# Products with v of two jobs in one group, queries turned by 24 rows, one PSUM bank for transposes

## The chip, the cores and the metric

The kernel runs on one core of one Trainium2 chip. The metric is the device time of one execution in microseconds, as the median of several runs. All times inside an execution come from one profiled execution, counted from the start of its span.

## The reference

Windowed attention with a few global keys feeds a gated feed-forward network. B = 4, H = 8 heads of D = 64, S = 768, d_model 512, d_ff 1024, all float32.

```python
rel = pos[:, None] - pos[None, :]
keep = (pos[None, :] < n_global) | ((rel >= 0) & (rel < n_local))   # 8 and 96
scores = q @ k.T / sqrt(D) - slopes[h] * dist                       # masked where not keep
x = softmax(scores) @ v                                             # heads side by side: 768 x 512
h = relu(x @ w_in)
conv = sum(conv_w[i] * shift(h, i) for i in range(3))               # along the sequence
out = (h * sigmoid(conv)) @ w_out
```

## The kernel before

A **job** is one batch, one half of the sequence (u = 0 or 1, 384 queries) and one pair of heads: 32 jobs. A job has three **steps** of 128 queries, 96 in all; the two heads of the pair are j = 0 and 1. Four jobs make the input x of one **unit** of the feed-forward network (FFN), so there are 8 units.

A step sees at most 232 keys: 96 before its 128 queries, its own 128, and 8 global ones. They stand in a first chunk of 128 (96 + 24 own + 8 global) and a second chunk of 104, the step's own keys 24 to 127. Queries 0 to 23 of a step see no key of the second chunk. The first step of a batch has 128 keys and no second chunk.

The way of one step, with its lines:

- L585 and L586 (L583 for the first nine jobs): scores into a PSUM bank, tile `s`, on TensorE.
- L594: bias, mask and maximum on VectorE, with a table `tab` made at the start from `rel`, the distances.
- L607: exponentials on ScalarE into `pbuf`, one of four buffers (`NPB`). L617 and L621: sum and reciprocal. L630 or L627: normalisation on VectorE, GpSimd or ScalarE.
- L639 and L640, `transposes`: second chunk and first chunk of each head are turned on TensorE into a PSUM bank `t`. There are two such banks, `tbank`, taken in turn. The weights are 104 or 128 columns of `pbuf`, and an identity of 128 columns is what moves. The second chunk is turned first and with all 128 queries, 24 more than it needs; the first chunk then overwrites those 24 columns.
- L646, `evict`: ScalarE copies the bank to one of four tiles `pt` (`NPT`) in SBUF.

After the three steps of a job, `values` (L656) multiplies with v into the one PSUM bank `pv`: for each step and chunk the two heads' weights are 64 columns wide and lie side by side; as fp32 each product is two instructions, 24 in a job and 20 in a job whose first step has one chunk. `high_x` (L666, ScalarE) and `low_x` (L671, VectorE) split the result into two fp32r parts, `xh` and `xl`, with six buffers each.

The FFN of a unit is `mm1` (L684, tile `h`, 3 matmuls of 384 columns for each of 8 x 4 blocks, which read the x of the unit's four jobs as k = 0 to 3), ReLU (L692), a three-tap convolution (L715 or L713, then L717 twice on VectorE), a gate (L725, L732, L749), a split (L756, L767) and `mm2` (L777, tile `o`, 3 matmuls of 512 columns for each of 8 blocks of a tile of rows). The last tile of rows is L805. The FFN's matmuls have a fixed order among themselves: the first layer of a unit (for its first two blocks all k in turn), then the second layer of the unit before.

The order in which each engine works is not written by hand. `fast_path` lists every operation with its engine, cost, buffers, predecessors and due time, and `Plan` places them one after another, by due time among those that are ready. `rooms` says how many buffers of a kind there are. In the first 40 us warm-up matmuls (L363) fill TensorE's gaps; by then the FFN's weights are decoded and split (L516 to L532). v (two buffers), q and k are loaded through SP's queue.

Of the kernel before, what the change touches and what calls it, by code (L numbers as in the profile page):

```python
# [23 lines left out]
P = 128  # L24
# [12 lines left out]

HF, NG = NF // 2, 4
NU, SPU = 2 * B, NPAIR * NB
NPB, NPT, NMM = 4, 4, 6  # L40
OFF = (1, 4)
NATIVE = 9
HK = 1024
# [33 lines left out]
class Plan:  # L77
# [53 lines left out]
    def arrange(self, free, taken):  # L131
# [31 lines left out]
                return min(max(0.0, port["DVE"] - t) * x, c[0] * x / (1 - x))  # L163
            return 0.0

        def room(b):

            t, n = b[0], self.rooms[b[0]]
            if queue[t][0] != b and t not in self.loose:
                return None  # L170
            ln = line.setdefault(t, [])
            if len(ln) < n:
                return 0.0
            old, at = ln[len(ln) - n]
            if old is None:
                return at
            return None if users[old] else gone[old]

        while cand:
            best = None  # L180
            heads = {}
            for k in cand:
                o = ops[k]
                at, ok = 0.0, True
                for b in o.alloc:
                    r = room(b)
                    if r is None:
                        ok = False
                        break
                    at = max(at, r)  # L190
                if not ok:
                    continue
                for a in o.after:
                    at = max(at, end[a])
                for e, c in o.eng.items():
                    t = max(free[e], at + WAKE[e])
                    if k[0] in LOADS:
                        t = max(t, landed[-LANES])
                    if e == "DVE" and last_max and k[0] == "max":
                        t = max(t, free[e] + 130)  # L200
                    late = at + WAKE[e] + (MARGIN[e] if free[e] > EASY else 0)
                    heads.setdefault(e, []).append((max(t, late), o.due, k, c, t))
            if not heads:
                raise RuntimeError(sorted(map(str, cand))[:40])
            pick = None
            for e, hs in heads.items():
                t0 = min(h[0] for h in hs)
                _, due, k, c, t = min((h for h in hs if h[0] <= t0 + SLACK[e]), key=lambda h: (h[1], h[0]))
                if len(ops[k].eng) > 1:
                    mine = t + c[0] + beside(e, c, t) + (c[2] if len(c) > 2 else 0)  # L210
                    others = [
                        h[4] + h[3][0] + beside(x, h[3], h[4]) + (h[3][2] if len(h[3]) > 2 else 0)
                        for x, g in heads.items() if x != e for h in g if h[2] == k
                    ]
                    if others and min(others) < mine:
                        hs = [h for h in hs if h[2] != k]
                        if not hs:
                            continue
                        t0 = min(h[0] for h in hs)
                        _, due, k, c, t = min((h for h in hs if h[0] <= t0 + SLACK[e]), key=lambda h: (h[1], h[0]))  # L220
                if pick is None or t < pick[0]:
                    pick = (t, e, k, c)
            t, e, k, c = pick
            o = ops[k]
            del cand[k]
            if k[0] in LOADS:
                free[e] = t + ISSUE
                wire = max(t + ISSUE + SETUP, wire) + c[0]
                end[k] = wire + RESULT["SP"]
                landed.append(end[k])  # L230
            else:
                cost = c[0] + beside(e, c, t)
                free[e] = t + cost
                end[k] = t + cost + (150 if k[0] == "max" else RESULT[e])
                if e == "POOL" and c[1]:
                    port[e], pool_op = t + cost, k
                if e == "DVE" and c[1] > 1:
                    port["slow"] = BESIDE[k[0]]
                    if port["POOL"] > t:
                        x = port["slow"]  # L240
                        more = min(cost * x, (port["POOL"] - t) * x / (1 - x))
                        port["POOL"] += more
                        free["POOL"] = max(free["POOL"], port["POOL"])
                        end[pool_op] += more
                    port[e] = t + cost
            if e == "DVE":
                last_max = k[0] == "max"
            done.append((t, o, e))
            for b in o.alloc:
                queue[b[0]].remove(b)  # L250
                line.setdefault(b[0], []).append((b, 0.0))
            for b in {*o.alloc, *o.use}:
                users[b] -= 1
                gone[b] = max(gone[b], end[k])
            for x in outs[k]:
                left[x] -= 1
                if not left[x]:
                    cand[x] = None
# [17 lines left out]
def fast_path(tc, io):  # L276
# [13 lines left out]
    px = pool("px", 6)  # L290
    pg = pool("pg", 4)
    ps_s = pool("ps_s", 2, space=PSUM)
    ps_t = pool("ps_t", 2, space=PSUM)
    ps_v = pool("ps_v", 1, space=PSUM)
    ps_m = pool("ps_m", 3, space=PSUM)
    p2 = pool("p2", 2)

# [22 lines left out]
    def load_q(m, j):  # L320
        b, u, hp = jobs[m]
        if m < NATIVE:
            r = slice(D * j, D * j + D)
            E = nc.sync if m + j else nc.scalar
            E.dma_start(raw[m, "q"][r, j * TB : j * TB + TB], io["qt"][b, hp, r, u * TB : u * TB + TB])
        else:
            t = raw[m, "q"] = p1.tile([P, 2 * TB], F32, tag="rq", name=f"rq{m}")
            nc.sync.dma_start(t, io["qk%d" % u][b, hp][:, : 2 * TB])
# [33 lines left out]
        for _ in range(n):  # L362
            T.matmul(wp[0][:, TB : TB + P], wz, wz, start=len(wp) > 1, stop=len(wp) > 1, skip_group_check=len(wp) == 1)  # L363

    tbank = [ps_t.tile([P, 2 * WIN], F32, tag="t", name=f"t{x}") for x in range(2)]
    for t in tbank:
        for c in range(0, 2 * WIN, P):
            w = min(P, 2 * WIN - c)
# [12 lines left out]
    for c0, n, base in pieces:  # L381
        if base is None:
            G.iota(reli[:, c0 : c0 + n], pattern=[[0, n]], base=-1, channel_multiplier=0)
        else:
            G.iota(reli[:, c0 : c0 + n], pattern=[[-1, n]], base=base, channel_multiplier=1)
    keyi = p2.tile([P, NGLOB], I32, tag="pt", name="keyi", bufs=NPT)
    G.iota(keyi, pattern=[[1, NGLOB]], base=0, channel_multiplier=0)
    ident = const.tile([P, P], F32, name="ident")
    V.tensor_copy(rel, reli)
    keyf = p1.tile([P, NGLOB], F32, tag="ob", name="keyf")  # L390
    V.tensor_copy(keyf, keyi)

# [67 lines left out]

    zero_q(0)
    make_identity(nc, ident)
    zero_q(1)

    cw = const.tile([P, 3 * NF], F32, name="cw")
# [166 lines left out]
    def transposes(s, j):  # L632
        n = form(s)[3]
        pb = pbuf[s % NPB]
        if j == 0:
            st_pt[s] = tbank[s % 2]
        pt, c = st_pt[s], j * WIN
        if n > P:
            T.transpose(pt[:NLATE, c + NLATE : c + WIN], pb[:, c + P : c + WIN], ident)  # L639
        T.transpose(pt[:, c : c + P], pb[:, c : c + P], ident)  # L640

    def evict(s):
        sb = p2.tile([P, 2, WIN], F32, tag="pt", name=f"pt{s}", bufs=NPT)
# [5 lines left out]
    def values(m):  # L649
        pv[m] = ps_v.tile([P, TB], F32, tag="v", name=f"pv{m}")  # L650
        for i in (NB - 1, *range(NB - 1)):
            whole = form(NB * m + i)[2]
            sb = st_pt.pop(NB * m + i)
            for c, n, q in ((0, P, 0),) if whole else ((0, P, 0), (1, NLATE, NEAR)):
                for j in range(2):
# [5 lines left out]
                        stop=c == 1 or whole,  # L661
                    )

    def high_x(m):
        xh = px.tile([P, TB], F32R, tag="xh", name=f"xh{m}")
        A.activation(xh, pv[m], AF.Copy)  # L666
        xt[m] = [xh, None]

    def low_x(m):
        xl = px.tile([P, TB], F32R, tag="xl", name=f"xl{m}")  # L670
        V.tensor_tensor(xl, pv[m], xt[m][0].bitcast(F32), ALU.subtract)  # L671
        xt[m][1] = xl

# [190 lines left out]
    def table_on(h, r, eng="DVE"):  # L864
        table(h, r, V if eng == "DVE" else G)

    plan = Plan(dict(s=2, t=2, v=1, m=3, xh=6, xl=6, gh=4, gl=4, rk=1, rq=1, kk=2, ql=2, qh=2,
                     vv=2, pt=NPT, pb=NPB, mm=6, c=1, ob=1), ("ob",))
    add = plan.add
    NRM_POOL, NRM_ACT, TAP_ACT = 300.0, 200.0, 0.0  # L870
# [11 lines left out]
    def due_of(s):  # L882
# [2 lines left out]
            return 8000 + i * PACE0  # L885
        return max(8000 + s * PACE0, starts[n - 1] + (i + 1) / SPU * spans[n - 1] - LEAD)

    for m in range(len(jobs)):
        native, w = m < NATIVE, NKC[jobs[m][1]]
        D0 = due_of(NB * m)  # L890
# [21 lines left out]
        for i in range(NB):  # L912
# [20 lines left out]
                add(("t", s, j), ("PE", (108 if first else 196, 0)), (transposes, s, j), [("nrm", s, j)],  # L933
                    (("t", s),) if j == 0 else (), (("t", s), ("pb", s)), d + 1500 + j, [("t", s, 0)] if j else [])
            add(("ev", s), act(256 if first else 2 * WIN), (evict, s), [("t", s, 0), ("t", s, 1)], (("pt", s),), (("t", s),), d + 2200)
        add(("pv", m), ("PE", (1570 if jobs[m][1] else 1390, 0)), (values, m), [("ev", NB * m + i) for i in range(NB)] + [("ldv", m)],
            (("v", m),), (("vv", m), *(("pt", NB * m + i) for i in range(NB))), d + 3000)
        ss = [("pv", m)]
        add(("xh", m), act(TB), (high_x, m), ss, (("xh", m),), (("v", m),), d + 3500)
        add(("xl", m), ("DVE", (TB * 1.042 + 68, 0)), (low_x, m), [("xh", m)], (("xl", m),), (("xh", m), ("v", m)), d + 3900)  # L940

# [249 lines left out]
def host(q, k, v, n_global, n_local, moe_w_in, moe_conv_w, moe_w_out):  # L1191
    arrays = {}
    qt = q.transpose(0, 1, 3, 2).reshape(B, NPAIR, 2, D, S).transpose(0, 1, 3, 2, 4)
    kt = k.transpose(0, 1, 3, 2).reshape(B, NPAIR, 2, D, S).transpose(0, 1, 3, 2, 4)
    for u in range(2):
        qu = qt[..., u * TB : (u + 1) * TB].reshape(B, NPAIR, D, 2 * TB)
        ku = kt[..., key_columns(u)].reshape(B, NPAIR, D, 2 * NKC[u])
# [12 lines left out]
    vv = vn[:, :, idx]  # L1210
    vv = vv.reshape(B, NPAIR, 2, NB, 2, P, P).transpose(0, 2, 1, 5, 3, 4, 6)
    arrays["vv"] = vv.reshape(B, 2, NPAIR, P, NB * 2 * P)
    arrays["qt"] = q.transpose(0, 1, 3, 2).reshape(B, NPAIR, P, S)
    arrays["kt"] = k.transpose(0, 1, 3, 2).reshape(B, NPAIR, P, S)
    arrays["vn"] = vn
# [25 lines left out]
```

## Time and profile before

| | before |
|---|---|
| median of 3 runs | 429.93 us (429.76 to 430.14) |
| profiled execution | 429.85 us, span 428.1 us |
| TensorE busy | 420.0 us, 98% |
| TensorE weight loads | 375.1 us, 88% |
| VectorE busy | 361.3 us, 84% |
| ScalarE busy | 311.5 us, 73% |
| GpSimd busy | 116.7 us, 27% |
| mean granted TensorE clock | 0.999 |
| chain that ended last | TensorE 57%, VectorE 33% |

Matmuls are pipelined: a row's duration holds the latency, and neighbouring rows overlap. What a matmul costs the engine is the distance from its start to the next start, the pitch. The last 55 us of the span (from 373) are the FFN of the last unit alone.

### The profile page before, as it was taken

The page shows a single profiled execution, that of the slowest core. Times are in us where ns is not written, and L with a number is a line of the kernel's source. Part 1 is how long each engine was busy: PE and PEld are TensorE (multiplying, and loading weights), DVE is VectorE, ACT ScalarE, POOL GpSimd, SP SyncE. Part 2 cuts the span into 40 slices and gives each one's busy share as a digit, 9 for nine tenths or more (in the row PEclk, how much of TensorE's full clock was granted, in tenths as well). Part 3 has the DMA queues.
Part 4 walks back from the last instruction along what each step waited for, and adds up shares of the span by engine and source line. Part 5 has one row for each costly group of instructions (what it writes and reads, how often), then busy time and mean ns, then how long its engine had stood idle before and what let it go on. Part 6 is the DMA issues. An engine that isn't in the chain of part 4 may idle for free.

```text
span 428.1 us, 8754 instructions
## 1 busy us (share of the span) xinstructions
PE 420.0 (98%) x2996; PEld 375.1 (88%) x2996; DVE 361.3 (84%) x1030; ACT 311.5 (73%) x829; POOL 116.7 (27%) x176
## 2 busy tenths in 40 slices
PE   8999999999999999999999999999999999999996
PEld 7999999898899778998799988899789988898885
DVE  7799999999899998889998997789999986568700
ACT  3789998989897885588878856589877886355511
POOL 6554444533213311223321421123203310001000
PEclk9999999999999999999999999999999999999999
DMA  7998544425403344434334323434444123576111
GB/s 254 301 339 281 174 141 154 143 85 160 143 31 123 112 147 113 139 97 148 96 117 123 86 90 105 156 114 124 122 160 129 57 70 116 198 266 224 51 49 54
DMA packets 22513, 59.85 MB, mean 140 GB/s; under 512 B 2880, under 2 KB 5440, under 8 KB 22464
## 3 DMA queue, kind: packets, MB, share of 16 engines
q1 hardware_dynamic: 21952, 58.89, 43.6%
q8 instruction: 24, 0.39, 0.4%
q10 hardware_dynamic: 512, 0.36, 0.3%
q14 instruction: 25, 0.20, 0.1%
HBM read 52.95 MB, written 6.29 MB: 138 GB/s over the span
## 4 chain that ended last, share of the span: by engine, by line
PE 57%; DVE 33%; issue 4%; ACT 4%; DMA 1%; POOL 0%; ACTq 0%; POOLq 0%
PE o L777 21%; PE h L684 17%; DVE c L717 8%; DVE s L594 6%; PE pv L656 5%; DVE kk L341 3%; DVE pbuf L630 3%; DVE c L749 3%; PE t L640 3%; PE s L583 2%; PE t L639 2%; DVE ql L349 2%; DVE gl L767 2%; PE s L586 2%; PE s L585 2%
## 5 line engine op out<-in xcount | busy, mean ns | idle before, releaser
L607 ACT ACTIVATE pbuf<-s,mm 128x232 f32<-128x232 f32 (+1 forms) x192 | 82.7, 437 | 33.3 <-DVE mm L594 32.8
L684 PE MATMUL h<-xh,wih 128*128 128x384 f32 x256 | 93.5, 365 | 0.0
L717 DVE SCALAR_TENSOR_TENSOR c<-hbuf,cw,c 128x382 f32<-128x382 f32 (+1 forms) x128 | 84.1, 673 | 3.4 <-POOL c L715 2.6
L684 PE MATMUL h<-xh,wil 128*128 128x384 f32 x256 | 86.5, 338 | 0.0
L684 PE MATMUL h<-xl,wih 128*128 128x384 f32 x256 | 86.5, 338 | 0.0
L594 DVE CUSTOM_DVE_ANT_0 s<-s,tab 128x232 f32<-128x232 f32 (+1 forms) x192 | 73.2, 381 | 10.6 <-PE s L586 7.1
L777 PE MATMUL o<-woh,gh 128*128 128x512 f32 x184 | 76.5, 416 | 0.0
L777 PE MATMUL o<-woh,gl 128*128 128x512 f32 x184 | 72.9, 396 | 0.0
L777 PE MATMUL o<-wol,gh 128*128 128x512 f32 x184 | 72.8, 396 | 0.0
L646 ACT ACTIVATE pt<-t 128x464 f32<-128x464 f32 (+1 forms) x96 | 50.8, 531 | 12.6 <-PE t L640 12.2
L715 POOL TENSOR_SCALAR c<-hbuf,cw 128x382 f32<-128x382 f32 (+1 forms) x33 | 24.9, 758 | 104.9 <-ACT hbuf L692 89.7
L684 PEld LDWEIGHTS h<-xh,wih 128*128 128x128 f32 x256 | 48.3, 189 | 1.4
L684 PEld LDWEIGHTS h<-xl,wih 128*128 128x128 f32 x256 | 48.4, 189 | 0.2
L684 PEld LDWEIGHTS h<-xh,wil 128*128 128x128 f32 x256 | 48.1, 188 | 0.0
L640 PE MATMUL t<-ident,pbuf 128*128 128x128 f32 x192 | 47.0, 275 | 0.1
L337 POOL CAST kk<-rk 128x1008 fp32r<-128x1008 f32 (+1 forms) x23 | 25.6, 1113 | 77.6 <-PE s L586 45.8
L656 PEld LDWEIGHTS pv<-pt,v 128*64 128x64 f32 (+1 forms) x704 | 36.1, 136 | 8.1 <-issue 4.0
L639 PE MATMUL t<-ident,pbuf 128*104 128x128 f32 x160 | 40.5, 278 | 2.4 <-DVE pbuf L630 2.1
L656 PE MATMUL pv<-pt,v 128*64 128x128 f32 (+1 forms) x704 | 42.5, 267 | 0.0
L777 PEld LDWEIGHTS o<-woh,gl 128*128 128x128 f32 x184 | 34.6, 188 | 8.2
L630 DVE TENSOR_SCALAR pbuf<-pbuf,mm 128x232 f32<-128x232 f32 (+1 forms) x109 | 40.4, 395 | 1.0
L777 PEld LDWEIGHTS o<-woh,gh 128*128 128x128 f32 x184 | 34.8, 189 | 6.0
(105 smaller groups left out, 843.0 us busy)
## 6 DMA issues: line engine op xcount, KB each, us to landing
v<-in_vv SPq DMA_DIRECT2D x32, 384.0 KB, 3.2
rq<-in_qk SPq DMA_DIRECT2D x23, 384.0 KB, 3.6
check<-in_w SPq DMA_DIRECT2D x16, 512.0 KB, 4.2
wr<-in_w SPq DMA_DIRECT2D x16, 511.6 KB, 5.8
rk<-in_qk SPq DMA_DIRECT2D x12, 504.0 KB, 3.5
out<-ob SPq DMA_DIRECT2D x23, 256.0 KB, 2.1
rk<-in_qk SPq DMA_DIRECT2D x11, 400.0 KB, 3.1
rq<-in_qt SPq DMA_DIRECT2D x17, 96.0 KB, 5.0
```

Source lines behind the costliest of these rows:

```text
L337: G.tensor_copy(kk, raw[m, "k"])
L594: V.tensor_tensor_reduce(out=o, in0=o, in1=tab[:, h, WIN:] if first else tab[:, h, 0:WIN], scale=-0.125, scalar=3.0e38, op0=ALU.add, op1=A ...
L607: last_exp[s] = A.activation(weights_of(s, j), st_s[s][:, j, :n], AF.Exp, bias=mm[:, j : j + 1], scale=-1.0, accum_out=mm[:, 2 + 2 * j : 3 ...
L630: X.tensor_scalar(x, x, y, 1.0, ALU.mult, ALU.mult)
L639: T.transpose(pt[:NLATE, c + NLATE : c + WIN], pb[:, c + P : c + WIN], ident)
L640: T.transpose(pt[:, c : c + P], pb[:, c : c + P], ident)
L646: A.activation(sb[:, :, :n], pt[:, :, :n], AF.Copy)
L656: T.matmul(pv[m][64 * j : 64 * j + 64, i * P + q : (i + 1) * P], vt[m][:n, i, c, 64 * j : 64 * j + 64], sb[:n, j, c * P : c * P + P - q], ...
L684: T.matmul(ps[:, :TB], w_[:, k, f * P : (f + 1) * P], x_, start=part == 0 and k == 0, stop=part == 2 and k == NK - 1,)
L715: G.tensor_scalar(c, h, x, 1.0, ALU.mult, ALU.mult)
L717: V.scalar_tensor_tensor(c, h, x, c, ALU.mult, ALU.add)
L777: T.matmul(ps, g_[:, f], w_[:, f], start=f == 0 and part == 0, stop=f == NF - 1 and part == 2,)
```

## The change

Queries of each step are turned by 24 rows: the host orders them 24 to 127, 0 to 23. The queries that see the second chunk then stand in rows 0 to 103, so its transposes take 104 rows and move an identity of 104 columns. The first chunk is turned with an identity that is turned too, which puts the queries back in order. The distances of the mask follow: `wrap` takes 128 from the rows from 104 on.

From job 8 on, the products with v of jobs 8 and 9, 10 and 11, and so on are one operation of the plan, which waits for the evictions of both jobs. `pv` gets a second bank, and the transposes keep one. `pbuf` goes from four buffers to three, `pt` from four to six, `xl` from six to five. The plan now counts buffers one by one where an operation takes two of a kind.

```diff
-NPB, NPT, NMM = 4, 4, 6
+NPB, NPT, NMM = 3, 6, 6
+XH, XL, SINGLE = 6, 5, 8
...
-    ps_t = pool("ps_t", 2, space=PSUM)
-    ps_v = pool("ps_v", 1, space=PSUM)
+    ps_t = pool("ps_t", 1, space=PSUM)
+    ps_v = pool("ps_v", 2, space=PSUM)
...
-            E.dma_start(raw[m, "q"][r, j * TB : j * TB + TB], io["qt"][b, hp, r, u * TB : u * TB + TB])
+            E.dma_start(raw[m, "q"][r, j * TB : j * TB + TB], io["qn"][b, hp, r, u * TB : u * TB + TB])
...
-    tbank = [ps_t.tile([P, 2 * WIN], F32, tag="t", name=f"t{x}") for x in range(2)]
+    tbank = [ps_t.tile([P, 2 * WIN], F32, tag="t", name=f"t{x}") for x in range(1)]
...
-            G.iota(reli[:, c0 : c0 + n], pattern=[[-1, n]], base=base, channel_multiplier=1)
+            G.iota(reli[:, c0 : c0 + n], pattern=[[-1, n]], base=base + NEAR, channel_multiplier=1)
+    rowi = p2.tile([P, 1], I32, tag="pt", name="rowi", bufs=NPT)
+    G.iota(rowi, pattern=[[0, 1]], base=0, channel_multiplier=1)
...
-    ident = const.tile([P, P], F32, name="ident")
-    V.tensor_copy(rel, reli)
+    eye = const.tile([P, P + NLATE], F32, name="eye")
+    ident, turned = eye[:, :P], eye[:, NLATE:]
+    wrap = const.tile([P, 1], F32, name="wrap")
+    V.tensor_scalar(wrap, rowi, float(NLATE), -float(P), ALU.is_ge, ALU.mult)
+    V.tensor_scalar(rel, reli, wrap, None, ALU.add)
...
     make_identity(nc, ident)
+    G.tensor_copy(eye[:, P:], eye[:, :NLATE])
...
-            st_pt[s] = tbank[s % 2]
+            st_pt[s] = tbank[s % len(tbank)]
         pt, c = st_pt[s], j * WIN
         if n > P:
-            T.transpose(pt[:NLATE, c + NLATE : c + WIN], pb[:, c + P : c + WIN], ident)
-        T.transpose(pt[:, c : c + P], pb[:, c : c + P], ident)
+            T.transpose(pt[:NLATE, c + P : c + WIN], pb[:NLATE, c + P : c + WIN], ident[:NLATE, :NLATE])
+        T.transpose(pt[:, c : c + P], pb[:, c : c + P], turned)
...
+    def products(group):
+        for m in group:
+            values(m)
...
-    plan = Plan(dict(s=2, t=2, v=1, m=3, xh=6, xl=6, gh=4, gl=4, rk=1, rq=1, kk=2, ql=2, qh=2,
+    plan = Plan(dict(s=2, t=len(tbank), v=2, m=3, xh=XH, xl=XL, gh=4, gl=4, rk=1, rq=1, kk=2, ql=2, qh=2,
...
+    groups = [[m] for m in range(SINGLE)] + [[m, m + 1] for m in range(SINGLE, len(jobs), 2)]
...
-        add(("pv", m), ("PE", (1570 if jobs[m][1] else 1390, 0)), (values, m), [("ev", NB * m + i) for i in range(NB)] + [("ldv", m)],
-            (("v", m),), (("vv", m), *(("pt", NB * m + i) for i in range(NB))), d + 3000)
-        ss = [("pv", m)]
+        group = next(g for g in groups if m in g)
+        if m == group[-1]:
+            add(("pv", group[0]), ("PE", (380 + sum(1190 if jobs[x][1] else 1010 for x in group), 0)), (products, group),
+                [k for x in group for k in (*(("ev", NB * x + i) for i in range(NB)), ("ldv", x))],
+                tuple(("v", x) for x in group),
+                tuple(k for x in group for k in (("vv", x), *(("pt", NB * x + i) for i in range(NB)))), d + 3000)
+        ss = [("pv", group[0])]
...
+    turn = np.arange(S).reshape(-1, P)
+    turn = np.roll(turn, -NEAR, axis=1).reshape(-1)
+    qt = qt[..., turn]
...
+    arrays["qn"] = q.transpose(0, 1, 3, 2).reshape(B, NPAIR, P, S)[..., turn]
```

The rest of the diff gives `xh` and `xl` their numbers of buffers and lets `Plan.room` count the buffers of one kind that one operation takes.

## Rows read from the trace of the kernel before

**Rows 1.** Busy us by stretch: window, length, PE, PEld, DVE, ACT, POOL, clock, DMA

```profile
40.00:155.00 115.00, 113.48 (x826) 102.30 (x824) 111.93 (x320) 101.24 (x276) 41.36 (x49) 1.00 0.41 130
155.00:193.00 38.00, 38.00 (x272) 34.40 (x271) 33.70 (x100) 26.73 (x76) 8.79 (x12) 1.00 0.43 125
210.00:285.00 75.00, 75.00 (x526) 66.93 (x524) 64.43 (x174) 53.91 (x141) 15.46 (x20) 1.00 0.40 121
285.00:326.00 41.00, 40.34 (x279) 36.04 (x278) 39.05 (x106) 32.34 (x92) 11.76 (x14) 1.00 0.37 111
326.00:373.00 47.00, 46.91 (x323) 40.59 (x324) 36.29 (x100) 32.22 (x82) 7.06 (x9) 1.00 0.37 115
```

**Rows 2.** Chain of waits, 210 to 285 (with one piece) and 285 to 326

```profile
by line: PE o L777 36.4%; PE h L684 33.5%; PE pv L656 10.3%; PE t L640 5.3%; PE s L586 5.1%; PE s L585 5.1%; PE t L639 4.9%
...
263.52 2.81 PE o L777 x12
...
by line: DVE c L717 12.0%; DVE s L594 11.1%; issue 10.8%; ACT pbuf L607 8.8%; DVE pbuf L630 7.9%; DVE kk L341 7.5%; DVE c L749 5.9%; DVE gl L767 5.9%; DVE ql L349 5.0%; ACT hbuf L692 3.7%; DVE mm L594 3.5%; ACT c L713 2.7%; DVE xl L671 2.6%
```

**Rows 3.** Timeline of TensorE, transposes: start, duration, instruction

```profile
16.48 0.27 PE L639 MATMUL t<-ident,pbuf 128*104 128x128 f32 x1
16.59 0.27 PE L640 MATMUL t<-ident,pbuf 128*128 128x128 f32 x1
...
19.69 0.27 PE L639 MATMUL t<-ident,pbuf 128*104 128x128 f32 x1
...
325.55 0.27 PE L639 MATMUL t<-ident,pbuf 128*104 128x128 f32 x1
```

**Rows 4.** Groups of instructions by shape, products with v: busy us, mean ns

```profile
L656 PE MATMUL pv<-pt,v 128*64 128x128 f32 x384 | 36.2, 280 | 0.0
...
L656 PE MATMUL pv<-pt,v 104*64 104x104 f32 x320 | 28.0, 252 | 0.0
```

**Rows 5.** Busy time by stretch, the second-chunk transposes (L639) alone

```profile
155.00:193.00 38.00, 3.62 (x15) 1.80 (x14) 1.00 0.43 125
210.00:285.00 75.00, 7.59 (x32) 3.87 (x30) 1.00 0.40 121
...
326.00:373.00 47.00, 4.87 (x19) 2.45 (x19) 1.00 0.37 115
```

**Rows 6.** Groups of instructions by shape, weight loads of the transposes

```profile
L640 PEld LDWEIGHTS t<-ident,pbuf 128*128 128x128 f32 x192 | 26.4, 141 | 5.8 <-ACT pbuf L627 0.8 <-POOL rq L304 0.2
...
L639 PEld LDWEIGHTS t<-ident,pbuf 128*104 128x104 f32 x160 | 20.6, 129 | 7.7 <-DVE pbuf L630 3.1 <-ACT c L725 1.0 <-ACT pbuf L627 0.8
```

**Rows 7.** Timeline of TensorE around one call of the products

```profile
258.60 0.39 PE L777 MATMUL o<-woh,gl 128*128 128x512 f32 x1
258.92 1.42 PE L656 MATMUL pv<-pt,v 128*64 128x128 f32 x24
260.26 0.50 PE L777 MATMUL o<-woh,gh 128*128 128x512 f32 x1
260.60 0.40 PE L777 MATMUL o<-wol,gh 128*128 128x512 f32 x1
```

**Rows 8.** Busy time by stretch, the products with v (L656) alone

```profile
155.00:193.00 38.00, 4.08 (x68) 3.47 (x68) 1.00 0.43 125
210.00:285.00 75.00, 8.16 (x136) 6.95 (x136) 1.00 0.40 121
...
326.00:373.00 47.00, 5.68 (x96) 4.87 (x96) 1.00 0.37 115
```

**Rows 9.** Timeline of ScalarE, exponentials of step 5 and two evictions

```profile
18.21 0.46 ACT L607 ACTIVATE pbuf<-s,mm 128x232 f32<-128x232 f32 x1
...
19.47 0.38 ACT L646 ACTIVATE pt<-t 128x256 f32<-128x256 f32 x1
...
325.91 0.57 ACT L646 ACTIVATE pt<-t 128x464 f32<-128x464 f32 x1
```

**Rows 10.** Timeline of GpSimd at the start

```profile
1.57 0.14 POOL L387 IOTA keyi<- 128x8 int32 x1
```

More of the change, by code (lines that the diff above doesn't have):

```diff
@@ L164, in beside, with room @@
             return 0.0
-        def room(b):
+        def room(b, k):
             t, n = b[0], self.rooms[b[0]]
-            if queue[t][0] != b and t not in self.loose:
+            if queue[t][k] != b and t not in self.loose:
                 return None
             ln = line.setdefault(t, [])
-            if len(ln) < n:
+            if len(ln) + k < n:
                 return 0.0
-            old, at = ln[len(ln) - n]
+            old, at = ln[len(ln) + k - n]
             if old is None:
@@ L184, in arrange @@
                 at, ok = 0.0, True
-                for b in o.alloc:
-                    r = room(b)
+                for x, b in enumerate(o.alloc):
+                    r = room(b, sum(y[0] == b[0] for y in o.alloc[:x]))
                     if r is None:
@@ L662, in values @@
                     )
+    def products(group):
+        for m in group:
+            values(m)
     def high_x(m):
-        xh = px.tile([P, TB], F32R, tag="xh", name=f"xh{m}")
+        xh = px.tile([P, TB], F32R, tag="xh", name=f"xh{m}", bufs=XH)
         A.activation(xh, pv[m], AF.Copy)
@@ L669, in low_x @@
     def low_x(m):
-        xl = px.tile([P, TB], F32R, tag="xl", name=f"xl{m}")
+        xl = px.tile([P, TB], F32R, tag="xl", name=f"xl{m}", bufs=XL)
         V.tensor_tensor(xl, pv[m], xt[m][0].bitcast(F32), ALU.subtract)
```

## The prediction

> **What bounds the kernel now.** I read the profile in this order: the busy times by stretch, the chain of waits by stretch, then the three groups of instructions that the change touches. After the first 40 us, which load and start, TensorE is busy for nearly all of every stretch, so the first reading is that TensorE sets the time and that any matmul slot saved is time saved. The second engine refines it. VectorE is busy 111.9 of 115 us from 40 to 155 and 39.1 of 41 from 285 to 326, but only 33.7 of 38, 64.4 of 75 and 36.3 of 47 in the three stretches that I call PE-led [rows 1]. The chain agrees: from 210 to 285 all of its lines are TensorE's, from 285 to 326 it runs through VectorE's taps, maxima and splits [rows 2]. The stretch from 193 to 210 I count to the VectorE-led ones, 40 to 155 too. So a shorter TensorE program is worth its full length in 155 to 193, 210 to 285 and 326 to 373 (160 us), something less in the other stretches up to 373, where VectorE has 2 to 5% left, and nothing after 373, where neither transposes nor products with v run.
>
> **The change, part by part.** Sums are made against the profiled execution, 429.85 us with a span of 428.1; the median is 429.93, 0.08 more, so differences carry over.
>
> *Second-chunk transposes, 128 to 104 moving columns.* There are 160. Two neighbouring transposes start 0.11 us apart, 16.48 and 16.59 [rows 3], whether the weights are 104 or 128 wide. That is about 0.85 ns a column, where the FFN's 512 columns take 0.234 us, 0.46 ns a column (12 in 2.81 us [rows 2]), at the same granted clock of 1.00. The nearest rows for fewer columns are the two forms of the products with v, also fp32: 280 ns with 128 moving columns, 252 with 104 [rows 4]. So 24 columns less are worth 24 x 0.85 = 20 ns by the pitch, 28 ns by the durations, and nothing if something else holds the pitch. I take 20 ns: the pitch is what the queue sees. In the PE-led stretches stand 15 + 32 + 19 = 66 such transposes [rows 5]: 66 x 0.02 = 1.3 us. The other 94 are worth 1.9 us at most.
>
> What could hold the pitch is the weight load of the first-chunk transpose, still 128 wide, which has to fit under a 104-column matmul. The rows speak against it: the load lasts 141 ns for 128 columns and 129 for 104 [rows 6], which is 12 ns for 24 columns, 0.5 ns a column, so 128 columns fill about 64 ns and the rest of the row is latency. The Trainium skill (TensorE: Matmul & The Clock Gate, section LDWEIGHTS) puts a weight load at its columns divided by 1.2 GHz, an estimate of 107 ns here; by that rule the pitch would stay at 107 ns and this part would give 0 instead of 3.2 us. The slope of the two rows is half of what the rule says.
>
> *Products of two jobs in one group.* One call stands at 258.92 to 260.26 [rows 7]. Coming from the FFN matmul before it, at 258.60, it starts 0.32 us later where that stream's pitch is 0.23: 0.09 lost. Its 24 matmuls run as 12 pairs, two heads beside each other on half the columns each: 6 x 0.11 + 6 x 0.09 = 1.20, against 1.34 taken: 0.14 lost. Going out, the first FFN matmul takes 0.34 instead of 0.23: 0.11 lost. So a call carries 0.34 us of switching between 64-column and full-width weights. The second job of a group should pay none of it, since nothing between two jobs differs from what already stands between two steps of one call; if the change of bank or of v tile cost as much as a switch, the gain would be 0. I take 0.34. Jobs 8 to 31 make 12 groups, so 4.1 us in all. In the PE-led stretches stand 68 + 136 + 96 instructions of that line [rows 8], 13 calls of 20 or 24, of which 6 become the second of a group: 2.0 us.
>
> PE-led gain: 1.3 + 2.0 = 3.3 us. Elsewhere: 1.9 + 2.1 = 4.0 us, between nothing (VectorE holds) and all (TensorE is 98 to 99% busy there too [rows 1]). I take half, 2.0, since both engines are nearly full and each small gap that either leaves moves the other.
>
> *Products moved later.* The first job's products wait for the second job's last eviction. What queues behind: its high and low parts of x on ScalarE and VectorE, and with them the first FFN layer of the unit, which is to find parts 0 and 1 ready but no longer part 2. Where a unit starts with FFN work in hand, other matmuls cover it. Where a VectorE-led stretch ends in a group (about 210 and 326) one call of 1.2 us can stand bare: between 0 and 2.4 us, and I take 1.2. The pair also holds both v buffers to its end, so the next two loads of v, and what stands behind them on SP's queue, start later; the plan orders that queue by the same waits, and the data is wanted only at the next pair's end. Cost 0, unless a q or k load is caught behind, which is in the range.
>
> *One transpose bank.* A step's transposes must now wait until ScalarE has evicted the step before. In 19 of the 95 neighbouring pairs of steps the transposes began before that eviction had ended: first at 19.69, with the eviction from 19.47 for 0.38, last at 325.55, with the eviction from 325.91 for 0.57 [rows 3, 9]. The other 76 are untouched. In the 19 the overlap is 0.16 us at the first and 0.93 at the last; at a mean of 0.55 it is 10 us if TensorE stood still each time. It need not: the order of TensorE is worked out again with one bank, and FFN matmuls can stand in between. I take 0, with 10 us as the other end.
>
> *Three probability buffers, six evicted tiles, five low parts.* With three buffers the exponentials of a step must follow the transposes three steps back; they already do at all 93 places, by 1.35 us at the closest (transposes from 16.59 for 0.27, exponentials at 18.21 [rows 3, 9]). Six tiles hold just one pair, so the next pair's first eviction follows the group; that is so already at all but one of the places, because the transposes come later anyway. Cost 0 for both, hidden by the present order.
>
> *Start.* One more index row on GpSimd (the small one beside it takes 0.14 [rows 10]), one tiny and one wider VectorE operation ahead of the first table, a copy for the widened identity: 0.2 us, between 0 (the first scores wait for q) and 0.5. Loads of q move the same bytes from another array.
>
> **Sum:** -3.3 - 2.0 + 1.2 + 0.2 = -3.9, so 429.85 goes to about 426.0, and the median with it.
>
> **Rivals.**
> *All of it shows.* TensorE really bounds every stretch, the re-made order hides the later products: -7.3 + 0.2 gives 422.8. For it: TensorE's 98 to 99% in the VectorE-led stretches. Against: VectorE's 95 to 97% there.
> *VectorE keeps its stretches.* The 4.0 us elsewhere vanish: -3.3 + 1.4 gives 428.0. For it the chain from 285 to 326.
> *The weight load holds the transposes at 0.11 us.* The 128-wide load behind a 104-column matmul then sets the pitch, and the groups alone count: 2.0 + 1.0 - 1.4 = 1.6, so 428.2. For it: the pitch is 0.11 now with both widths. Against: the slope of the load's rows [rows 6]. The rule of the Trainium skill given above would bring this about.
> *The single bank stalls TensorE: slower.* Evictions stand in ScalarE's queue behind other work: the one at 325.91 belongs to a step whose successor's transposes were already under way at 325.55. So the transposes of the next step reach a bank that is not free and hold back every matmul behind them. Price up to 10 us against the 4 gained; it decides from 0.04 us a step on, and at two thirds the time is 429.85 - 3.9 + 6.7 = 432.6. For it: the 19 overlaps. Against: 96 steps in some 360 us are one every 3.8, and a step's transposes (0.44) and eviction (0.57) fill a quarter of that.
> *Nothing happens:* the switch is paid between two jobs as well, the transposes' pitch does not follow the columns, and the later products are covered: 430.0 with the start's 0.2.
>
> **Chances.** Forecast 0.42; all of it 0.14; VectorE keeps 0.14; weight load 0.07; slower by the bank 0.16; nothing 0.07. A measurement here tells 0.2%, 0.86 us, from no change. The first four end below 429.1: faster 0.77; same 0.07; slower 0.16. The range from 422.8 to 431.0 takes in all but most of the slower case and the edge of the best one. The forecast's own range is 424.2 to 427.6.
>
> **What would show it.** Second-chunk transposes near 255 ns, with the transposes behind them starting 0.09 us on; 48-instruction groups of 2.5 us, with no step in the middle; TensorE's waits for ScalarE's eviction near nothing, and the 210-to-285 stretch shorter by 1.5 to 2 us. The prediction is wrong if transposes wait on the eviction for more than 4 us in all, if the stretches led by VectorE grow, or if TensorE stands idle ahead of the first FFN matmuls of a unit.

## The result and the profile after

The changed kernel takes 423.85 us (median of 4 runs, 422.92 to 424.52) against 430.03 us for the kernel before timed along with it: ratio 0.985, 95% interval 0.9839 to 0.9862, so 6.2 us faster. The forecast was 426.0, its range 422.8 to 431.0. The profiled execution took 422.92 us with a span of 421.1.

The engines in the page of the changed kernel, busy us and share of the span, then the number of instructions:

```profile
PE 413.5 (98%) x3021; PEld 372.0 (88%) x3021; DVE 358.8 (85%) x1023; ACT 308.5 (73%) x827; POOL 127.8 (30%) x188
```

TensorE is busy for 6.5 us less than before (420.0) and the span is 7.0 us shorter, so nearly all of what went is busy time of TensorE. (Busy time is not work alone: a row holds its latency too.) The timeline of TensorE in the changed kernel, one step's transposes and one group:

```profile
255.71 0.26 PE L646 MATMUL t<-eye,pbuf 104*104 104x104 f32 x1
255.81 0.27 PE L647 MATMUL t<-eye,pbuf 128*128 128x128 f32 x1
255.93 0.25 PE L646 MATMUL t<-eye,pbuf 104*104 104x104 f32 x1
256.02 0.27 PE L647 MATMUL t<-eye,pbuf 128*128 128x128 f32 x1
...
263.93 0.40 PE L788 MATMUL o<-woh,gl 128*128 128x512 f32 x1
264.25 2.62 PE L663 MATMUL pv<-pt,v 128*64 128x128 f32 x48
266.81 0.44 PE L647 MATMUL t<-eye,pbuf 128*128 128x128 f32 x2
```

The transposes' pitch, 0.11 throughout in [rows 3], is now 0.09 to 0.10 after a second chunk and 0.11 to 0.12 after a first one; unrounded, as medians over the whole trace, 92 and 112 ns where it was 109 and 109. A pair of chunks costs 204 ns instead of 218. The 48 matmuls of a group take 2.56 us to the next start, two single calls of 24 took 2 x 1.34 [rows 7], and one entry (0.32 against a pitch of 0.23) and one exit are saved besides. By shape (busy us, mean ns, idle time before):

```profile
L646 PE MATMUL t<-eye,pbuf 104*104 104x104 f32 x160 | 37.9, 259 | 2.1 <-ACT pbuf L634 0.7 <-DVE pbuf L637 0.6 <-ACT pt L653 0.6
L663 PE MATMUL pv<-pt,v 128*64 128x128 f32 x384 | 35.6, 277 | 0.0
L663 PE MATMUL pv<-pt,v 104*64 104x104 f32 x320 | 28.0, 252 | 0.0
```

What TensorE waited for, in all, times and longest:

```profile
PE t L370 <- POOL setup L356: 1.0, 1, 1.0
PE t L646 <- ACT pbuf L634: 0.7, 2, 0.6
PE t L646 <- DVE pbuf L637: 0.6, 2, 0.3
PE t L646 <- ACT pt L653: 0.6, 2, 0.4
PE s L590 <- DMA rq<-in_qn: 0.4, 1, 0.4
PE t L647 <- ACT pt L653: 0.2, 1, 0.2
```

Three transposes wait for an eviction (`pt`), 0.8 us in all: that is what the single bank costs TensorE here. No first-layer matmul (`h`) waits for a part of x. The chain of waits still runs through VectorE in some stretches and through TensorE alone in others, but the borders have moved. It is VectorE's from 40 to 114 and TensorE's from 306 to 366 (first two lines). From 114 on it is TensorE's too (third line, 114 to 180):

```profile
by line: DVE c L728 18.0%; DVE s L601 16.8%; issue 10.9%; DVE pbuf L637 7.4%; DVE kk L342 7.1%; DVE wol L539 6.3%; DVE ql L350 6.1%; DVE w L528 5.8%; DVE gl L778 4.6%; DVE xl L682 3.9%; DVE mm L601 3.7%; DVE mm L628 2.0%; DVE c L760 1.9%; D
...
by line: PE o L788 42.6%; PE h L695 28.0%; PE pv L663 12.1%; PE t L647 4.8%; PE t L646 4.4%; PE s L593 4.1%; PE s L592 4.0%
...
by line: PE h L695 34.4%; PE o L788 34.0%; PE pv L663 11.0%; PE t L647 5.6%; PE s L593 5.4%; PE s L592 5.2%; PE t L646 4.6%
```

In the kernel before VectorE led there; its chain from 114 to 155:

```profile
by line: DVE c L717 27.6%; DVE s L594 9.6%; DVE gl L767 8.7%; DVE c L749 8.6%; DVE kk L341 8.3%; issue 8.2%; DVE ql L349 6.4%; ACT sat L732 4.8%; DVE pbuf L630 2.4%; DVE xl L671 2.2%; ACT pbuf L607 2.1%; ACT c L725 2.1%; DVE mm L594 1.9%; D
```

### The profile page after: what moved, and what is told of

Its sections match the earlier page's. It is cut to its first block, busy times and chain, and to the rows that moved or that the text cites. A ratio compares the mean times of both kernels' runs of the same rounds, so it can differ in the third digit from the quotient of the medians.

```text
span 421.1 us, 8863 instructions
## 1 busy us (share of the span) xinstructions
PE 413.5 (98%) x3021; PEld 372.0 (88%) x3021; DVE 358.8 (85%) x1023; ACT 308.5 (73%) x827; POOL 127.8 (30%) x188
## 4 chain that ended last, share of the span: by engine, by line
PE 52%; DVE 33%; ACT 7%; issue 5%; POOL 1%; DMA 1%; ACTq 0%; DVEq 0%
PE o L788 21%; PE h L695 14%; DVE c L728 7%; DVE s L601 6%; PE pv L663 4%; DVE pbuf L637 3%; DVE c L760 3%; DVE kk L342 3%; PE t L647 2%; DVE ql L350 2%; ACT pbuf L614 2%; PE t L646 2%; PE s L593 2%; PE s L590 2%; PE s L592 2%
## 5 line engine op out<-in xcount | busy, mean ns | idle before, releaser
L695 PE MATMUL h<-xh,wih 128*128 128x384 f32 x256 | 92.1, 360 | 0.0
L728 DVE SCALAR_TENSOR_TENSOR c<-hbuf,cw,c 128x382 f32<-128x382 f32 (+1 forms) x128 | 82.7, 669 | 4.7 <-POOL c L726 2.9
L788 PE MATMUL o<-woh,gh 128*128 128x512 f32 x184 | 75.1, 408 | 0.0
L726 POOL TENSOR_SCALAR c<-hbuf,cw 128x382 f32<-128x382 f32 (+1 forms) x36 | 27.3, 764 | 84.3 <-ACT hbuf L703 81.6
L637 POOL TENSOR_SCALAR pbuf<-pbuf,mm 128x232 f32<-128x232 f32 (+1 forms) x36 | 26.6, 740 | 84.9 <-DVE mm L628 65.6
L647 PE MATMUL t<-eye,pbuf 128*128 128x128 f32 x192 | 45.7, 276 | 0.2 <-ACT pt L653 0.2
L637 DVE TENSOR_SCALAR pbuf<-pbuf,mm 128x232 f32<-128x232 f32 (+1 forms) x101 | 39.1, 405 | 1.1
L646 PE MATMUL t<-eye,pbuf 104*104 104x104 f32 x160 | 37.9, 259 | 2.1 <-ACT pbuf L634 0.7
L663 PE MATMUL pv<-pt,v 128*64 128x128 f32 (+1 forms) x704 | 39.9, 266 | 0.0
```

What stands on the lines that cost most here:

```text
L637: X.tensor_scalar(x, x, y, 1.0, ALU.mult, ALU.mult)
L646: T.transpose(pt[:NLATE, c + P : c + WIN], pb[:NLATE, c + P : c + WIN], ident[:NLATE, :NLATE])
L647: T.transpose(pt[:, c : c + P], pb[:, c : c + P], turned)
L663: T.matmul(pv[m][64 * j : 64 * j + 64, i * P + q : (i + 1) * P], vt[m][:n, i, c, 64 * j : 64 * j + 64], sb[:n, j, c * P : c * P + P - q], ...
L695: T.matmul(ps[:, :TB], w_[:, k, f * P : (f + 1) * P], x_, start=part == 0 and k == 0, stop=part == 2 and k == NK - 1,)
L726: G.tensor_scalar(c, h, x, 1.0, ALU.mult, ALU.mult)
```

## Experiments

Three readings of a gain above the forecast had to be told apart. Theory 1: a TensorE slot counts in full in every stretch. Theory 2: VectorE holds the stretches that it leads, as the prediction half assumed. Theory 3, of the order: an edit that changes what the plan knows makes it lay out another order, and the order alone moves the time.

To compare all runs I count, in each trace, TensorE's slots: each matmul at its usual pitch, the lower quartile of the distances between the same three neighbours over all 14 traces, warm-up matmuls left out. The rest of the span is start, warm-up and waiting. How high the sum comes out depends on the way of counting; a difference between two kernels holds to about 1 us. Each ratio is to the kernel before as timed along with that run; its medians were 430.0 to 431.0 us.

| run | median us | ratio to before, 95% interval | slots us | rest us |
|---|---|---|---|---|
| before (span 428.1) | 430.0 | | 391.9 | 36.1 |
| changed | 423.85 | 0.985, 0.9839 to 0.9862 | 384.8 | 36.3 |
| turned queries alone | 429.72 | 0.9987, 0.9979 to 0.9996 | 389.2 | 38.9 |
| groups alone | 424.08 | 0.9857, 0.9842 to 0.9871 | 387.5 | 34.7 |
| buffers alone | 431.08 | 1.0021, 1.0012 to 1.0029 | 391.3 | 37.4 |
| changed, two tiles | 423.23 | 0.9836, 0.9823 to 0.9848 | 384.6 | 37.3 |
| six groups, VectorE-led | 425.89 | 0.9878, 0.9863 to 0.9893 | 386.6 | 39.0 |
| six groups, PE-led | 424.43 | 0.9851, 0.9836 to 0.9866 | 386.5 | 36.3 |
| changed, lead 8800 | 423.26 | 0.9814, 0.9801 to 0.9828 | 384.8 | 36.8 |
| before, lead 8800 | 427.54 | 0.9919, 0.9905 to 0.9932 | 392.0 | 33.4 |
| before, lead 9200 | 428.05 | 0.9956, 0.9943 to 0.997 | 392.3 | 33.7 |
| before, TensorE more, early | 432.14 | 1.0049, 1.0035 to 1.0063 | 396.1 | 34.2 |
| before, TensorE more, middle | 433.24 | 1.0079, 1.0065 to 1.0093 | 396.0 | 35.3 |
| before, VectorE more, early | 435.27 | 1.0119, 1.0103 to 1.0134 | 392.1 | 42.0 |

**The turned queries alone.** Against the changed kernel:

```diff
-NPB, NPT, NMM = 3, 6, 6
-XH, XL, SINGLE = 6, 5, 8
+NPB, NPT, NMM = 4, 4, 6
+XH, XL, SINGLE = 6, 6, 32
...
-    eye = const.tile([P, P + NLATE], F32, name="eye")
-    ident, turned = eye[:, :P], eye[:, NLATE:]
+    ident = const.tile([P, P], F32, name="ident")
+    turned = const.tile([P, P], F32, name="turned")
```

with two banks for transposes and one for products (cut here).

> Only the turned queries and the 104-column transposes; two transpose banks, one product call for each job and all buffers as before; the identity and the turned identity stand in tiles of their own. Theory 1 (TensorE's slots set the time in every stretch): 160 transposes x 15 to 20 ns, 2.4 to 3.2 us faster than before, 427.0 to 427.6. Theory 2 (VectorE holds the stretches that it leads): only the 66 in the other stretches count, 1.0 to 1.3 us faster, 428.6 to 429.0. Theory 3 (weight loads hold the pitch): no change.

0.5 us faster (0.2 to 0.9 by the interval), though the slots shrank by 2.7: the rest of the span grew by as much. The order is no reason here. The plan reckons with the same cost for a transpose, and in the two traces the instructions of all engines stand in the same order, but for a few at the start. So the two evictions of [rows 9], at 19.47 and 325.91 before, can be compared:

```profile
19.72 0.38 ACT L654 ACTIVATE pt<-t 128x256 f32<-128x256 f32 x1
...
326.21 0.57 ACT L654 ACTIVATE pt<-t 128x464 f32<-128x464 f32 x1
```

Between them lie 136 of the shorter transposes, 1.9 us of TensorE at 14 ns each, and the later eviction is 326.21 - 325.91 - 0.25 = 0.05 us later, not earlier: in this pair of traces nothing of the saving shows. Part of it went into longer waits for VectorE's normalisation, 3.0 us in this trace and 2.1 before:

```profile
PE t L647 <- DVE pbuf L638: 3.0, 5, 0.8
```

```profile
PE t L639 <- DVE pbuf L630: 2.1, 4, 0.7
```

That weight loads hold the pitch (theory 3 of this expectation) is refuted: the pitch is 92 and 112 ns here too. None of the stated times came out.

**The groups alone.** The changed kernel with the queries in order (the distances of the mask and the host's order go back as well, cut here):

```diff
-            T.transpose(pt[:NLATE, c + P : c + WIN], pb[:NLATE, c + P : c + WIN], ident[:NLATE, :NLATE])
-        T.transpose(pt[:, c : c + P], pb[:, c : c + P], turned)
+            T.transpose(pt[:NLATE, c + NLATE : c + WIN], pb[:, c + P : c + WIN], ident)
+        T.transpose(pt[:, c : c + P], pb[:, c : c + P], ident)
```

> Only the groups of two jobs with their buffers (one transpose bank, two product banks, three probability buffers, six evicted tiles, five low parts); queries in order and transposes of 128 columns as before, the identity in the widened tile of after. Theory 1: 12 switches x 0.34 us, 4.1 us faster, 425.8. Theory 2: 6 of the 12, 2.0 us faster and less what the later products cost, 428.0 to 429. If the single bank stalled TensorE, slower than that. If the pitch of the transposes in the changed kernel (112 ns after a first chunk, 109 before) comes from the widened tile, it is 112 here too.

6.1 us faster, 2.0 more than theory 1 allowed: 4.4 us of slots and 1.4 of rest are gone. So something beside the slots was gained. This kernel and the changed one have the same order too, but for a few instructions at the start; 424.08 against 423.85, and against 423.23 for the changed kernel with two tiles (below), so the shorter transposes are worth 0.2 to 0.9 us here as well. The pitch is 109 ns, with the identity in the widened tile.

**The buffers alone.** The kernel before with (cut here: the PSUM pools and `xl` follow these numbers)

```diff
-NPB, NPT, NMM = 4, 4, 6
+NPB, NPT, NMM = 3, 6, 6
...
-    plan = Plan(dict(s=2, t=2, v=1, m=3, xh=6, xl=6, gh=4, gl=4, rk=1, rq=1, kk=2, ql=2, qh=2,
+    plan = Plan(dict(s=2, t=1, v=2, m=3, xh=6, xl=5, gh=4, gl=4, rk=1, rq=1, kk=2, ql=2, qh=2,
```

> The kernel before with the changed kernel's buffers alone: one transpose bank, two product banks, three probability buffers, six evicted tiles, five low parts; no groups, transposes as before. If the single bank costs nothing, as the prediction took it: 429.5 to 430.5. If it stalls TensorE: slower by up to 10 us, with transposes waiting for evictions.

0.9 us slower. Of TensorE's waits two have to do with an eviction, 0.2 us each:

```profile
PE t L639 <- ACT pbuf L627: 1.4, 3, 0.8
...
PE pv L656 <- ACT pt L646: 0.2, 1, 0.2
PE t L639 <- ACT pt L646: 0.2, 1, 0.2
```

The single bank does not stall TensorE. The groups alone, with the same buffers, are 7.0 us faster than this kernel.

**Two tiles for the identities.** The changed kernel with the two `const.tile` lines of the diff under the turned queries alone, and copies that fill them.

> The changed kernel with the identity and the turned identity in two tiles instead of one widened tile. If the widened tile costs the transposes 3 ns each (352 of them), 1 us faster than the changed kernel, near 422.8, and pitches of 89 and 109 ns. If the 3 ns come from the 104 rows or the alternation of widths, the same time as the changed kernel, 423.9, and pitches of 92 and 112.

423.23 us, within the spread of the changed kernel, with pitches of 92 and 113 ns. The 3 ns come with the turned pair itself and not with the widened tile.

**Six groups of the twelve.** The changed kernel with

```diff
-    groups = [[m] for m in range(SINGLE)] + [[m, m + 1] for m in range(SINGLE, len(jobs), 2)]
+    paired = (8, 10, 12, 16, 24, 26)   # the other run: (14, 18, 20, 22, 28, 30)
+    groups = [[m] for m in range(SINGLE)]
+    for m in range(SINGLE, len(jobs), 2):
+        groups += [[m, m + 1]] if m in paired else [[m], [m + 1]]
```

> The changed kernel, but only the six groups whose second call stood in stretches led by VectorE before are kept (jobs 8, 10, 12, 16, 24, 26 with their neighbours); the other jobs from 8 on are called singly, all buffers as in the changed kernel. Theory 1: half of the switches are saved, 6 x 0.34 = 2.0 us slower than the changed kernel, 425.9. Theory 2: these groups are worth nothing, so as slow as no groups at all, 4 us over the changed kernel less what is left, 426.5 to 428, and slower than the kernel with the other six groups.

> The other six groups alone (jobs 14, 18, 20, 22, 28, 30 with their neighbours), whose second call stood in stretches led by TensorE before. Theory 1: 425.9, the same as with the six of the stretches led by VectorE. Theory 2: these are the ones that count, so near the changed kernel, 424 to 425, and 2 us faster than the kernel with the other six.

425.89 and 424.43: the six PE-led groups are 1.5 us faster with the same slots (386.6 and 386.5). That is theory 2's direction, but the two kernels have different orders, and the runs below show that an order alone can do as much. By itself it decides nothing.

**Another order of the same instructions.** The lead is a number of the plan, by how much attention is due ahead of the network. In each kernel

```diff
-    T0, PACE0, LEAD, TAPS = 36000.0, 2000.0, 9000.0, 18000.0
+    T0, PACE0, LEAD, TAPS = 36000.0, 2000.0, 8800.0, 18000.0
```

and, for the kernel before, 9200 as well.

> The changed kernel with one number of the plan changed, the lead of attention over the network from 9000 to 8800, which makes another order of the same instructions. It measures what a re-made order alone moves: if within 0.5 us of the changed kernel, the gain can be put down to the saved slots; if it moves by 2 us or more, part of the gain is the luck of the order.

> The kernel before with the same one number of the plan changed, 9000 to 8800. As for the changed kernel: within 0.5 us of 430.0 if the order is of little weight, 2 us or more away if it counts.

> The kernel before with the lead of attention over the network at 9200 instead of 9000: a third order of the same instructions, beside 430.0 at 9000 and 427.5 at 8800. If the order at 9000 is an unlucky one, 427 to 428; if the order at 8800 is a lucky one, 429.5 to 430.5.

The changed kernel hardly moves: 423.26. The kernel before gets faster with either: 427.54 at 8800 and 428.05 at 9200. Its slots are the same 392; the rest of the span falls from 36.1 to 33.4 and 33.7. TensorE's waits for normalised probabilities (2.1 us for VectorE and 0.2 for ScalarE in the kernel before) show part of it; at 8800 and then at 9200:

```profile
PE t L639 <- ACT pbuf L627: 1.0, 2, 0.7
```

```profile
PE t L639 <- DVE pbuf L630: 0.9, 3, 0.4
```

So the order in which the kernel before ran is the worst of the three tried: against the kernel before as timed along with each, 8800 is faster by 3.4 us (430.98) and 9200 by 1.9 (429.99), and by the spans it is 2.6 and 2.1. At a lead of 8800 the two kernels, timed on the same chip, stand at 423.26 and 427.54: the change is worth 4.3 us there.

**A slot more in one stretch, order unchanged.** These three kernels keep the order of every engine, since the plan does not know of the additions:

```diff
         T.transpose(pt[:, c : c + P], pb[:, c : c + P], ident)
+        if 24 <= s < 42:                    # the other run: 58 <= s < 76
+            T.transpose(pt[:, c : c + P], pb[:, c : c + P], ident)
```

and, for VectorE, after each maximum

```diff
+        if 24 <= s < 42:
+            V.tensor_copy(junk, ident)
```

> The kernel before with its order unchanged, but in steps 24 to 41 (about 70 to 155 us, led by VectorE) each first-chunk transpose is issued twice, the second time onto the same place: 36 matmuls of 0.109 us, 3.9 us of TensorE. Theory 1 (a TensorE slot counts in full in every stretch): 3.5 to 4 us slower than before, 433.6 to 434.2. Theory 2 (VectorE holds this stretch): at most half shows, 430 to 432.

> The same 36 extra matmuls in steps 58 to 75 (about 209 to 283 us, led by TensorE). Both theories: 3.5 to 4 us slower than before, 433.6 to 434.2. It is the yardstick for the same addition in the stretch led by VectorE.

> The kernel before with its order unchanged, but in steps 24 to 41 each maximum is followed on VectorE by a copy of 128 columns of the identity into a tile that nobody reads: 36 copies of 0.1 to 0.2 us, 4 to 7 us of VectorE. Theory 1: VectorE is nearly full there but TensorE is what counts, so less than half shows, 430 to 432. Theory 2: VectorE holds the stretch, so all of it shows, 434 to 437.

The same two evictions of [rows 9], which there start at 19.47 and 325.91, can be found in each; between them lie all the additions. TensorE more in the stretch led by VectorE:

```profile
19.86 0.39 ACT L648 ACTIVATE pt<-t 128x256 f32<-128x256 f32 x1
...
328.19 0.57 ACT L648 ACTIVATE pt<-t 128x464 f32<-128x464 f32 x1
```

TensorE more in the stretch led by TensorE:

```profile
19.48 0.38 ACT L648 ACTIVATE pt<-t 128x256 f32<-128x256 f32 x1
...
329.28 0.57 ACT L648 ACTIVATE pt<-t 128x464 f32<-128x464 f32 x1
```

VectorE more in the stretch led by VectorE, with the copy itself (minimum, median and longest ns):

```profile
20.32 0.38 ACT L649 ACTIVATE pt<-t 128x256 f32<-128x256 f32 x1
...
331.97 0.57 ACT L649 ACTIVATE pt<-t 128x464 f32<-128x464 f32 x1
```

```profile
L601 DVE COPY junk<-ident x36: 216/222/868, 67.8 to 141.5; 128x128 f32<-128x128 f32 x36
```

Less what the start already differed by, the late eviction moved by 328.19 - 325.91 - 0.39 = 1.9 us, by 3.4, and by 331.97 - 325.91 - 0.85 = 5.2. The medians of whole runs say nearly the same: 2.2, 3.3 and 5.3 us over the kernel before timed along with them (429.99). TensorE was given 36 x 0.109 = 3.9 us each time: about half shows in the VectorE-led stretch (49% by the evictions, 55% by the medians) and 86% or 83% in the PE-led one. VectorE was given at least 36 x 0.138 = 5.0 us, by the copies' median pitch (some took longer), and 5.2 shows. For added work theory 1 falls, and so does theory 2 in its strict form: in that stretch a VectorE slot counts in full or nearly, and a TensorE slot by half. That each engine waits for the other in turn would explain it; that is argued, not shown. A slot added need not count like a slot saved: of the 2.2 us that the shorter transposes save in an unchanged order, 0.2 to 0.9 shows.

## Why the prediction held, and where it was off

The direction and the range held, in part by luck: two parts were off in opposite ways. The forecast gave the transposes 1.3 + half of 1.9 = 2.3 us and the groups, less the later products, 2.0 + half of 2.1 - 1.2 = 1.9. Taken alone the transposes give 0.2 to 0.9 us and the groups with their buffers 6.1. The steps:

- *Transposes.* Mis-sized twice. The slot: 20 ns forecast, 14 measured (17 saved after a second chunk, 3 lost after a first), 2.2 us instead of 3.2. And its worth: in an order that stays as it is, 0.2 to 0.9 us of these 2.2 show. By the Trainium skill's rule for weight loads (TensorE: Matmul & The Clock Gate, section LDWEIGHTS), an estimate of 107 ns for 128 columns, the pitch after a second chunk would have stayed at 107 ns. The trace disagrees: it is 92. That the load does not hold the pitch at 0.11 was right, but the reason given for it was weak. The 0.5 ns a column, taken from the two rows of [rows 6], is not a rate: the loads of the products with v, 64 columns wide, last longer than the 129 ns of 104 columns.

```profile
L656 PEld LDWEIGHTS pv<-pt,v 128*64 128x64 f32 x384 | 21.0, 135 | 8.1 <-issue 4.0 <-ACT pt L646 1.8 <-ACT pbuf L607 1.0
```

- *Switching.* Right: two calls of 24 took 2 x 1.350 = 2.70 us inside and one group 2.55, so 0.15 inside, 0.09 and 0.11 at the ends, 0.35 against 0.34.
- *What the groups are worth.* Too low. The 12 switches make 12 x 0.35 = 4.2 us, and 6.1 came. So at least 1.9 us is not switching; the table has 1.4 less of rest there. How much of the 4.2 shows as time is not known, since the groups have an order of their own.
- *Slots in all.* 7.1 us (391.9 to 384.8) by the table, 2.2 + 4.2 = 6.4 from the parts, against 7.3 forecast. With the rest at 36.1 and 36.3 this looks as if every slot had counted in full, the rival that ends at 422.8. The runs of the parts speak against it: the transposes' slots hardly show, and the groups gave more than theirs.
- *Half of what lies in the VectorE-led stretches, all of it elsewhere.* For slots added in an order held fixed it is 49% and 86%. For the transposes' saved slots it was too high: the 66 in the PE-led stretches, at 14 ns, would make 0.9 us in full, the upper end of what shows, and nothing is left for the other 94.
- *Later products, 1.2 us.* A term that did not come: no first-layer matmul waits for a part of x in the changed kernel. With the six VectorE-led groups only, two such waits show, 0.9 us in all, and at a lead of 8800 one of 0.3, so the mechanism exists.
- *Single bank and fewer buffers, 0 (up to 10 us).* 0.8 us of waits for an eviction in the changed kernel, 1.4 at a lead of 8800; 0.9 us slower when the buffers were changed alone, order included. The slower rival is refuted.
- *Where the gain fell.* Add up TensorE's instructions in their order, each at its pitch in the kernel before, and ask when each kernel reaches the sum that the kernel before has at a given time. This is good to about 1.2 us, since one call of products can stand on either side of a border. At 40 us the turned queries alone are 0.2 us behind, as forecast for the start, buffers alone 2.6 and the changed kernel 1.8. So the buffers, put at 0, cost about 2 us there. Buffers alone makes this up by 155 with no slot saved: with the new order the chain from 114 to 155 runs through TensorE there too. The changed kernel is ahead by 1.4 us at 155, 3.6 at 210, 4.2 at 285 and 6.5 at 373; the stretch from 210 to 285 became 0.6 us shorter and not 1.5 to 2.
- *What the prediction did not have.* An order alone moves the kernel before by 1.9 to 3.4 us. Between the forecast (-3.9) and the result (-6.2) lie 2.3 us, and an order's part is enough for them; at a lead of 8800 the change is worth 4.3, close to the forecast. But that the changed kernel won by its order is argued, not shown. Its rest, 36.3, is no lower than that of the kernel before, and how ordinary its order is rests on two orders (423.85 and 423.26).

Open stays how the 6.1 us of the groups divide into saved switches and a better order, and why so little of the shorter transposes shows. Longer waits for normalised probabilities, 3.0 us against 2.1, are part of the second; a change of order is not, since the order is the same.

## What to carry to other kernels

When a planner lays out the order, an edit can change two things: the work, and the order. Count the work in slots of the fullest engine, and measure the order by moving one harmless number of the plan in both kernels, before a gain of 1% is put down to the edit. To price a slot, keep the order: change the work without telling the plan, and compare the traces to see that the order is the same. Do not take the price of an added slot for that of a saved one: here about half of the added TensorE slots showed where VectorE was over 95% busy, and 10 to 40% of those saved by the transposes over the whole span. Price the parts one by one: a sum can come out right from two parts that are wrong in opposite ways. Small products on half the columns are worth putting one after another, since each call here paid 0.35 us of switching.

## What was unexpected of the hardware

The transpose with 104 rows, 104 weights and 104 moving columns starts the next one after 92 ns instead of the 89 that 104/128 of the old pitch gives, and the full transpose before it takes 112 instead of 109. With the same weights but 128 rows and 128 moving columns it was 109 both ways, in the widened tile too. The cause of the 3 ns was not tried further. A call on half the columns costs TensorE 0.35 us beside its matmuls, more than three of the half-column pairs (0.09 to 0.11 us each). The row of a weight load does not tell by its length how many columns were loaded: 135 ns for 64, 129 for 104 and 141 for 128, all fp32.
